# One pair of w_out products spread over both halves of the array around a batch's kv, and 32 columns of numerators in a round of their own

## The chip, the cores and the metric

The kernel runs on one core of a Trainium2 chip. The metric is the device time of one execution in microseconds (us), the median of the runs. Engines: TensorE (PE, with its weight loads as PEld), VectorE (DVE), ScalarE (ACT), GpSimd (POOL) and SyncE (SP, here only DMA issues).

## The reference: linear attention, then a gated feed-forward block

For each of 4 batches and 4 heads, 1088 tokens of 32 dimensions: q and k are mapped by two sketches S1 and S2 (8 rows each) to a = S1 x and b = S2 x, and phi(x) holds their 64 products. Then

```
kv  = sum over s of phi(k) v          # 64 x 32 a head
z   = sum over s of phi(k)            # 64 a head
out = (phi(q) kv) / (phi(q) z + 1e-6)
x   = out, as 4352 tokens x 128
y   = (sigmoid(x w_gate) * (x w_val)) w_out     # 128 -> 1536 -> 128
```

All is in f32.

## The kernel before, in words

**The feed-forward block is the stream that runs through the kernel.** The 4352 tokens are cut into chunks of 512 (`tok_chk`), the hidden 1536 into 12 blocks of 128. A *wave* (`w1`, L529 to L605) makes one block's gate and value products for one chunk in a PSUM tile `wave` (two buffers): from chunk 1 on each of the two is split into two products of 64 output rows (L542 to L544), so that two run side by side in the two halves of the array, one in its low 64 columns and one in its high 64. ACT takes the sigmoid (L552), and `glu` multiplies on DVE (L587). `slot` (L613) is the planner: for each wave it first finishes the wave before it (`glu`), then does the w_out products that are due (`todo`, due 3 and 4 waves after their pair), then issues the next wave. The calls from L1314 to the end write out by hand between which waves the attention's steps of the next batch stand, by wave numbers in `plan`.

**The w_out products.** From chunk 1 on, two hidden blocks form a pair (i = 0 to 5), and a 2 by 2 scheme with seven products replaces eight: POOL makes sums of the token halves (`token_sums`, tile `tsum`), `ws` holds sums of weights. `w2_a` (L468) issues three or four products of a pair into PSUM bank `fst["a"]`, one wave later `w2_b` (L495) the rest, mostly into bank `fst["b"]`. All have 64 output rows: `lo` is rows 0 to 63 of a bank and runs in the low half of the array, `hi` is rows 64 to 127 and runs in the high half; the rhs has 256 columns (`HALF`). For an even pair `w2_a` issues lo (L475), hi (L476), lo (L477); `w2_b` lo, hi, lo, hi. For an odd pair `w2_a` issues lo, hi, lo, hi and `w2_b` hi, lo, hi. So an even pair's first round gives the low half one product more, and the odd pair's second round gives it back to the high half. The products of a round stand right ahead of a wave on PE.

**The attention of batches 1 to 3**, each step between two waves: `begin` (kps, cqps: the sketches of k and q), `outer` and `sum_z` on DVE (phi(k) and its sum), then `kv_all` (L1310): 36 products of 64 columns and 4 more for z, in four groups of 32 output rows, over the whole array (L900, L909). In batch 1, kv stands between pair 0's `w2_a`, one wave, and pair 0's `w2_b`. Later `parts(b)` (L1276) makes numerators and denominators:

- `den_j` (L1026): eight products of 160 columns into the PSUM tile `denj` (buffer "two", one of its kind). The operands have 64 rows and the output 32, so that eight tiles of the array (two row halves, four column groups) work side by side. Between them stand eight numerator products of the last 32 columns, into the same tile at columns 160 to 191.
- DVE multiplies the sums by A8 into `pd` (L1047).
- eight numerator products of 512 columns into `nps`, a `wave` buffer (L1280 to L1282), copied out by ACT (L1285).
- `den_i` (L1051): two products of 160 columns from `pd` back into `denj`, whose columns 0 to 159 pd has read by then.
- DVE turns and inverts the denominators (`turn_den`) and multiplies the numerators by them into xT (L1302), the 32 last columns from `denj`.

Of the kernel before, what the change touches and what calls it, by code (L numbers as in the profile page):

```python
# [8 lines left out]
F32 = mybir.dt.float32  # L9
# [7 lines left out]
P = 128  # L17
# [3 lines left out]
def kernel(  # L21
# [12 lines left out]
    nc = tc.nc  # L34

    B, H, S, D = q.shape
# [26 lines left out]
    ps2 = ctx.enter_context(tc.tile_pool(name="ps2", bufs=1, space=bass.MemoryType.PSUM))  # L63
# [13 lines left out]
    W1 = 32 * q_chk[1][1]  # L77
# [111 lines left out]
    HALF = TCH // 2  # L189
    ws = const.tile([P, 4, NJ // 2, 64], F32, tag="ws", name="ws")  # L190
# [129 lines left out]
    for c in range(2):  # L320
        rows = slice(64 * c, 64 * c + 64)
        nc.vector.tensor_reduce(
            out=m_col[rows, c],
# [4 lines left out]
    for t, x in (  # L328
# [5 lines left out]
        out=e_sum,  # L334
# [45 lines left out]
    def product(out, lhsT, rhs, start, stop):  # L380
        nc.tensor.matmul(  # L381
            out=out, lhsT=lhsT, rhs=rhs, start=start, stop=stop, skip_group_check=True
        )
# [78 lines left out]
    fst = {}  # L462
# [2 lines left out]

    def w2_a(ci, i, g, t):  # L468
        if i == 0:
            moe["sum"] = ci  # L470
            fst["a"] = pso.tile([P, TCH], F32, tag="acc0", name="prod")
        ps = fst["a"]
        lo, hi = ps[:64], ps[64:]
        w, first, last = w_sb[:, 2], i == 0, i == NJ // 2 - 1
        product(lo[:, :HALF], w[:, 2 * i, :64], g[:, 0, :HALF], first, last)  # L475
        product(hi[:, :HALF], ws[:, 1, i], t[:, 2], first, last)  # L476
        product(lo[:, HALF:], ws[:, 3, i], g[:, 1, HALF:], False, last)  # L477
        if i % 2:
            product(hi[:, HALF:], ws[:, 2, i], t[:, 1], False, last)
        if last:  # L480
            e = fst["e"] = raw.tile([P, 4, HALF], F32, tag="w_in", name="other")
            r = fst["r"] = raw.tile([P, 3, HALF], F32, tag="w_in", name="res")
            nc.scalar.copy(out=e[:64, 0], in_=hi[:, :HALF])
            nc.scalar.copy(out=e[64:, 0], in_=lo[:, :HALF])  # L484
            add(r[:, 0], ps[:, :HALF], e[:, 0])
            add(r[:, 0], ps[:, HALF:], r[:, 0])
            moe["copies"] += [
                lambda: nc.scalar.copy(out=e[:64, 1], in_=lo[:, :HALF]),
                lambda: nc.scalar.copy(out=e[64:, 1], in_=r[64:, 0]),
            ]  # L490
# [4 lines left out]
    def w2_b(ci, i, g, t):  # L495
        if i == 0:
            fst["b"] = pso.tile([P, TCH], F32, tag="acc1", name="prod")
        ps = fst["b"]
        lo, hi = ps[:64], ps[64:]
        w, first, last = w_sb[:, 2], i == 0, i == NJ // 2 - 1  # L500
        p5 = (lo[:, HALF:], ws[:, 0, i], t[:, 0], False, last)
        p4 = (hi[:, :HALF], w[:, 2 * i + 1, 64:], t[:, 3], first, last)
        out2 = hi[:, HALF:] if i % 2 else lo[:, :HALF]
        p2 = (out2, w[:, 2 * i + 1, :64], g[:, 1, :HALF], first, i >= NJ // 2 - 2)
        p7 = (fst["a"][64:, HALF:], ws[:, 2, i], t[:, 1], False, False)
        for p in (p4, p5, p2) if i % 2 else (p2, p7, p5, p4):
            product(*p)
        if last:
            e, r = fst["e"], fst["r"]
            nc.scalar.copy(out=e[:64, 3], in_=hi[:, HALF:])  # L510
            o_sb = sbA.tile([P, TCH // 32, 32], F32, tag="o_sb", name="o_sb")

            add(r[:, 1], ps[:, :HALF], e[:, 1])
            add(r[:64, 1], r[:64, 1], e[:64, 3])
            moe["copies"] += [
                lambda: nc.scalar.copy(out=e[:64, 2], in_=lo[:, HALF:]),
                lambda: nc.scalar.copy(out=e[64:, 2], in_=lo[:, HALF:]),
            ]

            def turn_store():  # L520
                nc.vector.transpose(
                    out=o_sb.rearrange("p t x -> p (t x)"),
                    in_=r[:, 1:3].rearrange("p u x -> p (u x)"),
                )
                store(ci, lambda g4: o_sb[32 * g4 : 32 * g4 + 32])

            moe["late"] += [lambda: add(r[:, 2], r[:, 0], e[:, 2]), turn_store]
# [140 lines left out]
    WD = 160  # L668
# [352 lines left out]
        )  # L1021

    def den_j(b):  # L1026
        t = ps2.tile([P, 2, 512], F32, tag="two", name="denj")
        rest = t[:, :, WD : WD + 32]

        def sum_j(pi, x):  # L1030
            rows = slice(64 * pi, 64 * pi + 64)
            nc.tensor.matmul(  # L1032
                out=t[32 * x : 32 * x + 32, pi, :WD],
                lhsT=ZW[b][rows, 4 * (x % 2) : 4 * (x % 2) + 4].rearrange("p x i -> p (x i)"),
                rhs=B8[b][rows, (W1 - WD) * (x // 2) : (W1 - WD) * (x // 2) + WD],
                start=True,
                stop=True,
            )

        for x in range(4):  # L1040
            sum_j(0, x)
            numerator(b, rest, x, 1, True)
        for x in range(4):
            sum_j(1, x)
            numerator(b, rest, x, 0, True)
        PD[b] = sbA.tile([P, 2, WD], F32, tag="pd", name="pd", bufs=1)
        nc.vector.tensor_tensor(out=PD[b], in0=t[:, :, :WD], in1=A8[b], op=MUL)  # L1047
        return t


    def den_i(b, dps):  # L1051
        for pi in range(2):
            nc.tensor.matmul(  # L1053
                out=dps[64 * pi : 64 * pi + 64],
                lhsT=mask["head"].rearrange("p m x -> p (m x)"),
                rhs=PD[b][:, pi, :],
                start=True,
                stop=True,
            )
        return dps  # L1060

    def turn_den(b, dps):
        nt, over = WD // 32, (W1 - WD) // 32
        dT = sbA.tile([P, nt, 32], F32, tag="dTi", name="dTi", bufs=1)
        nc.vector.transpose(out=dT.rearrange("p t c -> p (t c)"), in_=dps)
        RC[b] = sbA.tile([P, 2, W1 // 32, 2], F32, tag="rci", name="rci")
        for t0, t1, u0, k in ((0, nt, 0, 0), (nt, W1 // 32, nt - over, 4)):
            nc.vector.tensor_scalar_add(
                RC[b][:, :, t0:t1],
                dT[:, u0 : u0 + t1 - t0, k : k + 4].rearrange("p t (n c) -> p n t c", n=2),  # L1070
                1e-6,
            )
        nc.vector.reciprocal(out=RC[b], in_=RC[b])
# [79 lines left out]
    else:  # L1153
        nc.vector.tensor_copy(
            out=s4[:, 1:],
# [106 lines left out]
        glu()  # L1262
        late.append(dn(0, 1)(later=True))

    def numerator(b, t, h, c, rest):
        rows = slice(64 * c, 64 * c + 64)
        q1 = QP[b].rearrange("p (n h w) -> p n h w", n=2, h=H)[rows, :, 2 * (h % 2) + h // 2]
        nc.tensor.matmul(  # L1268
            out=t[32 * h : 32 * h + 32, c],
            lhsT=ND[b][rows, 32 * h : 32 * h + 32],  # L1270
            rhs=q1[:, 1, W1 - 32 :] if rest else q1[:, :, : W1 - 32],
            start=True,
            stop=True,
        )

    def parts(b):  # L1276
        t2 = den_j(b)
        glu()
        t = psm.tile([P, 2, 512], F32, tag="wave", name="nps")
        for h in range(H):  # L1280
            for c in range(2):
                numerator(b, t, h, c, False)  # L1282
        num = sbA.tile([P, 2, NJK, 2, F], F32, tag="kp", name="num", bufs=1)
        num = num.rearrange("p c j m f -> p (c j m f)")[:, :1024].rearrange("p (c w) -> p c w", c=2)
        nc.scalar.copy(out=num, in_=t)  # L1285
        turn_den(b, den_i(b, t2[:, 0, :WD]))
        for n in range(2):
            rb = sbA.tile([P, 9, 2, 32], F32, tag="rb", name="rb")
            t0, tn = q_chk[n]
            r0 = RC[b][:, n]  # L1290
            nc.vector.transpose(
                out=rb[:, :tn].rearrange("p t c s -> p (t c s)"),
                in_=bass.AP(
                    tensor=r0.tensor,
                    offset=r0.offset,
                    ap=[list(r0.ap[0]), [1, 2 * tn], [0, 32]],
                ),
            )
            for u0, u1, x in ((0, 8, num[:, :, 256 * n : 256 * n + 256]), (8, tn, t2[:, :, WD : WD + 32])):
                if u0 < u1:  # L1300
                    o = b * S + 64 * (t0 + u0)
                    nc.vector.tensor_tensor(  # L1302
                        out=xT[:, o : o + 64 * (u1 - u0)].rearrange("p (t c s) -> p c t s", c=2, s=32),
                        in0=x.rearrange("p c (t s) -> p c t s", s=32),
                        in1=rb[:, u0:u1].rearrange("p t c s -> p c t s"),
                        op=MUL,
                    )
        moe["ready"] = b * S + S
# [102 lines left out]
```

## Time and profile before

| what | value |
|---|---|
| median of 3 runs | 290.91 us (290.83 to 291.48) |
| the profiled execution's own time | 291.36 us |
| its span, first to last instruction | 289.3 us |
| PE busy | 283.5 us, 98% of the span |
| POOL, DVE, ACT busy | 159.6, 170.8, 106.6 us |
| granted TensorE clock | 1.00 |
| waves (L544), 820 records | 201.9 us, mean 566 ns |
| w_out products (L381), 588 records | 168.6 us, 379 to 380 ns each |

An f32 product leaves two records, one for each of two passes over its columns. A record's duration holds the time from a pass's start until its last result; the next pass on the same part of the array starts earlier than that, so the distance between starts is what a pass occupies. Records of the two halves overlap in time, which is why the two lines' busy times add up to more than the span. A timeline row with a count (x7) merges records of one line that follow each other.

### The profile page before, as it was taken

Reading aid. Unit: us, or ns where it says so; the run is one execution under the profiler, and the core shown is the slowest. Engines: PE = TensorE matmul, PEld = TensorE weight load, DVE = VectorE, ACT = ScalarE, POOL = GpSimd, SP = SyncE. Lnnn points to the kernel's source line nnn. Section 1 sums busy time; section 2 is a strip of 40 time slices with the busy share of each in tenths; the row PEclk is TensorE's granted clock in tenths of the full one; section 3 lists DMA queues with packets and bytes.
Section 4 is the critical chain, followed back from the end, with each engine's and each line's share of the span. In section 5 each row is a group of like instructions: output and inputs, shape, how many; then the busy total and the mean of one; then the engine's idle time right before and its main releaser. Section 6 shows DMA issues by size and latency. Waiting matters only on the chain.

```text
span 289.3 us, 5786 instructions
## 1 busy us (share of the span) xinstructions
PE 283.5 (98%) x2260; PEld 134.9 (47%) x2260; DVE 170.8 (59%) x294; ACT 106.6 (37%) x215; POOL 159.6 (55%) x222
## 2 busy tenths in 40 slices
PE   8799999999999999999999999999999999999995
PEld 4454433354444444544444444444444444444685
DVE  6987788946738547668346385767245223522571
ACT  3688833222334322533234222522243223421341
POOL 2566673667466377372665396483564646555200
PEclk9999999999999999999999999999999999999999
DMA  7995541665600386442000683010001100020012
GB/s 216 343 361 120 111 155 42 164 147 135 186 11 2 77 187 162 105 156 37 0 1 6 157 162 128 2 28 10 0 3 18 18 2 0 3 35 1 0 17 40
DMA packets 28890, 24.22 MB, mean 84 GB/s; under 512 B 18560, under 2 KB 24064, under 8 KB 28864
## 3 DMA queue, kind: packets, MB, share of 16 engines
q1 hardware_dynamic: 25888, 22.10, 30.1%
q10 hardware_dynamic: 2976, 1.77, 2.1%
q8 instruction: 17, 0.28, 0.4%
q14 instruction: 9, 0.07, 0.1%
HBM read 20.60 MB, written 3.26 MB: 82 GB/s over the span
## 4 chain that ended last, share of the span: by engine, by line
PE 97%; ACT 1%; DVE 1%; issue 0%; POOL 0%
PE wave L544 61%; PE prod L381 22%; PE moeout L425 4%; PE moeout L451 2%; PE warm L301 2%; PE kvz L900 1%; PE nps L1268 1%; PE kps L681 1%; PE cqps L827 1%; PE nps L1101 0%; PE dps L1082 0%; PE denj L1053 0%; PE denj L1032 0%; ACT asb L798 0%; DVE qp L807 0%; PE ndps L965 0%
## 5 line engine op out<-in xcount | busy, mean ns | idle before, releaser
L544 PE MATMUL wave<-xT,w_sb 128*64 128x512 f32 (+3 forms) x820 | 201.9, 566 | 0.0
L552 ACT ACTIVATE sg<-wave 128x512 f32<-128x512 f32 x102 | 60.9, 597 | 158.6 <-PE wave L544 152.6
L587 DVE TENSOR_TENSOR g<-wave,sg 128x512 f32<-128x512 f32 x96 | 66.1, 688 | 88.2 <-ACT sg L552 87.6
L371 POOL TENSOR_TENSOR tsum<-g,tsum 128x256 f32<-128x256 f32 x84 | 68.4, 815 | 71.6 <-DVE g L587 71.5
L544 PEld LDWEIGHTS wave<-xT,w_sb 128*64 128x64 f32 (+1 forms) x820 | 71.3, 140 | 72.8 <-issue 53.0
L371 POOL TENSOR_TENSOR tsum<-g 128x256 f32<-128x256 f32 x84 | 66.4, 791 | 22.6 <-DVE g L587 22.0
L381 PE MATMUL prod<-tsum,ws 128*64 128x256 f32 x252 | 68.3, 380 | 0.0
L381 PE MATMUL prod<-g,w_sb 128*64 128x256 f32 x168 | 50.2, 380 | 0.0
L381 PEld LDWEIGHTS prod<-tsum,ws 128*64 128x64 f32 x252 | 34.0, 137 | 13.1 <-issue 9.7
L381 PEld LDWEIGHTS prod<-g,w_sb 128*64 128x64 f32 x168 | 22.7, 137 | 30.0 <-issue 25.8
L381 PE MATMUL prod<-tsum,w_sb 128*64 128x256 f32 x84 | 25.1, 380 | 0.0
L381 PE MATMUL prod<-g,ws 128*64 128x256 f32 x84 | 25.0, 379 | 0.0
L162 POOL TENSOR_TENSOR head<-head,tail 128x384 int32<-128x384 int32 (+1 forms) x13 | 13.2, 1021 | 4.4 <-DVE head L157 4.4
L381 PEld LDWEIGHTS prod<-g,ws 128*64 128x64 f32 x84 | 11.5, 137 | 5.7
L425 PE MATMUL moeout<-g,w_sb 128*128 128x512 f32 (+1 forms) x28 | 12.4, 600 | 0.0
L381 PEld LDWEIGHTS prod<-tsum,w_sb 128*64 128x64 f32 x84 | 11.3, 137 | 1.3 <-issue 1.0
L760 DVE TENSOR_TENSOR kp<-kab 128x1152 f32<-128x1152 f32 (+2 forms) x10 | 10.7, 1082 | 0.0
L580 DVE TENSOR_TENSOR g<-wave,sg 128x512 f32<-128x512 f32 x6 | 7.0, 1172 | 6.1 <-ACT sg L552 4.6
L880 DVE TENSOR_TENSOR qp<-qp,bq 128x1152 f32<-128x1152 f32 (+1 forms) x7 | 10.1, 1444 | 0.0
L493 DVE TENSOR_TENSOR res<-prod,other 128x256 f32<-128x256 f32 x14 | 6.0, 425 | 6.3 <-ACT other L484 4.8
L141 POOL TENSOR_SCALAR head<-cap 128x384 f32<-128x384 f32 (+1 forms) x13 | 6.3, 487 | 5.0 <-ACT cap L140 5.0
L152 ACT ACTIVATE tail<-w_in,two__157 128x384 f32<-128x384 uint32 (+1 forms) x12 | 7.3, 614 | 0.0
(132 smaller groups left out, 200.2 us busy)
## 6 DMA issues: line engine op xcount, KB each, us to landing
qp<-dq SPq DMA_DIRECT2D x7, 576.0 KB
bq<-dq SPq DMA_DIRECT2D x14, 288.0 KB
kq<-in_k_dram SPq DMA_DIRECT2D x3, 544.0 KB
kq<-in_q_dram SPq DMA_DIRECT2D x3, 544.0 KB
w_in<-in_moe_w_out_dram SPq DMA_DIRECT2D x6, 256.0 KB
w_in<-in_moe_w_gate_dram SPq DMA_DIRECT2D x5, 256.0 KB
w_in<-in_moe_w_val_dram SPq DMA_DIRECT2D x5, 256.0 KB
v<-in_v_dram SPq DMA_DIRECT2D x8, 144.0 KB
```

The costliest lines, as they stand in the source:

```text
L141: nc.gpsimd.tensor_scalar(out=self.head.bitcast(F32), in0=self.cap, scalar1=122880.0, scalar2=2.0**-15, op0=ALU.min, op1=ALU.max,)
L152: nc.scalar.activation(out=self.tail, in_=self.lo, func=ACTF.Identity, bias=two, scale=2.0**-51)
L162: nc.gpsimd.tensor_tensor(out=self.head, in0=self.head, in1=self.tail.bitcast(I32), op=ALU.add)
L371: nc.gpsimd.tensor_tensor(out=t[:, u], in0=in0, in1=in1, op=ALU.subtract)
L381: nc.tensor.matmul(out=out, lhsT=lhsT, rhs=rhs, start=start, stop=stop, skip_group_check=True)
L425: nc.tensor.matmul(out=moe["acc"][d], lhsT=w_sb[:, 2, j, d], rhs=g[:, jj], start=(j == 0), stop=(j == NJ - 1),)
L544: nc.tensor.matmul(out=wv[d, which, jj * tw + o : jj * tw + o + tp], lhsT=w_sb[:, which, j0 + jj, d], rhs=xT[:, t0 + o : t0 + o + tp], sta ...
L552: nc.scalar.activation(out=sg, in_=wv[:, 0], func=ACTF.Sigmoid)
L580: nc.vector.tensor_tensor(out=g.rearrange("p (j u s y) -> p j y u s", j=2, u=2, y=4), in0=wv[:, 1].rearrange("p (j y u s) -> p j y u s", j ...
L587: nc.vector.tensor_tensor(out=g, in0=wv[:, 1], in1=sg, op=MUL)
L760: eng.tensor_tensor(out=KP[b][:, pi, j0:j1].rearrange("p j m (i l) -> p (j m) i l", i=R), in0=bass.AP(tensor=a0.tensor, offset=a0.offset, ...
L880: nc.vector.tensor_tensor(out=q0, in0=q0, in1=half(BQ[b], n), op=MUL)
```

## The change

In `w2_a` the third product (L477) is left out for pair 0 of chunk 1. In `w2_b` that pair gets an order of its own: p2, the product into `lo[:, :HALF]`, is cut into two pieces of 128 columns, the second of which goes to the high half (`hi[:, HALF + x:]`, which is added to the low half's result at the end in any case), and the left-out product p3 is issued here, into `fst["a"]`. In `parts`, the eight numerator products of 32 columns no longer stand between the sums of `den_j`: they come after the 512-column numerators and their copy, in a new tile of the buffer "two", which `den_i` then writes too.

```diff
@@ w2_a
-        product(lo[:, HALF:], ws[:, 3, i], g[:, 1, HALF:], False, last)
+        if ci > 1 or i > 0:
+            product(lo[:, HALF:], ws[:, 3, i], g[:, 1, HALF:], False, last)
@@ w2_b
-        for p in (p4, p5, p2) if i % 2 else (p2, p7, p5, p4):
+        order = (p4, p5, p2) if i % 2 else (p2, p7, p5, p4)
+        if ci == 1 and i == 0:
+            w21, x = w[:, 1, :64], HALF // 2
+            p3 = (fst["a"][:64, HALF:], ws[:, 3, 0], g[:, 1, HALF:], False, False)
+            p2s = [
+                (lo[:, :x], w21, g[:, 1, :x], True, False),
+                (hi[:, HALF + x :], w21, g[:, 1, x:HALF], False, False),
+            ]
+            order = (p2s[0], p7, p3, p4, p5, p2s[1])
+        for p in order:
             product(*p)
@@ den_j
-        for x in range(4):
-            sum_j(0, x)
-            numerator(b, rest, x, 1, True)
-        for x in range(4):
-            sum_j(1, x)
-            numerator(b, rest, x, 0, True)
+        for pi in range(2):
+            rows = slice(64 * pi, 64 * pi + 64)
+            for x in range(4):
+                nc.tensor.matmul(...)
@@ numerators (was numerator, one product a call)
+    def numerators(b, t, rest):
+        for h in range(H):
+            for c in range(2):
...
@@ parts
-        t2 = den_j(b)
+        den_j(b)
         glu()
         t = psm.tile([P, 2, 512], F32, tag="wave", name="nps")
-        for h in range(H):
-            for c in range(2):
-                numerator(b, t, h, c, False)
+        numerators(b, t, False)
...
         nc.scalar.copy(out=num, in_=t)
-        turn_den(b, den_i(b, t2[:, 0, :WD]))
+        t = ps2.tile([P, 2, 512], F32, tag="two", name="nps2")
+        numerators(b, t[:, :, WD : WD + 32], True)
+        turn_den(b, den_i(b, t[:, 0, :WD]))
...
-            for u0, u1, x in (..., (8, tn, t2[:, :, WD : WD + 32])):
+            for u0, u1, x in (..., (8, tn, t[:, :, WD : WD + 32])):
```

The sum products in `den_j` and the numerator products themselves are the same as before; only their places and the tile of the 32-column ones differ.

More of the change, by code (lines that the diff above doesn't have):

```diff
@@ L1027, in den_j @@
         t = ps2.tile([P, 2, 512], F32, tag="two", name="denj")
-        rest = t[:, :, WD : WD + 32]
-        def sum_j(pi, x):
+        for pi in range(2):
             rows = slice(64 * pi, 64 * pi + 64)
[L1032 to L1038, printed above, removed]
-        for x in range(4):
-            sum_j(0, x)
-            numerator(b, rest, x, 1, True)
-        for x in range(4):
-            sum_j(1, x)
-            numerator(b, rest, x, 0, True)
+            for x in range(4):
+                nc.tensor.matmul(
+                    out=t[32 * x : 32 * x + 32, pi, :WD],
+                    lhsT=ZW[b][rows, 4 * (x % 2) : 4 * (x % 2) + 4].rearrange("p x i -> p (x i)"),
+                    rhs=B8[b][rows, (W1 - WD) * (x // 2) : (W1 - WD) * (x // 2) + WD],
+                    start=True,
+                    stop=True,
+                )
         PD[b] = sbA.tile([P, 2, WD], F32, tag="pd", name="pd", bufs=1)
         nc.vector.tensor_tensor(out=PD[b], in0=t[:, :, :WD], in1=A8[b], op=MUL)
-        return t
     def den_i(b, dps):
@@ L1263, in part01 @@
         late.append(dn(0, 1)(later=True))
[L1265 to L1274, printed above, removed]
+    def numerators(b, t, rest):
+        for h in range(H):
+            for c in range(2):
+                rows = slice(64 * c, 64 * c + 64)
+                q1 = QP[b].rearrange("p (n h w) -> p n h w", n=2, h=H)[rows, :, 2 * (h % 2) + h // 2]
+                nc.tensor.matmul(
+                    out=t[32 * h : 32 * h + 32, c],
+                    lhsT=ND[b][rows, 32 * h : 32 * h + 32],
+                    rhs=q1[:, 1, W1 - 32 :] if rest else q1[:, :, : W1 - 32],
+                    start=True,
+                    stop=True,
+                )
     def parts(b):
-        t2 = den_j(b)
+        den_j(b)
         glu()
         t = psm.tile([P, 2, 512], F32, tag="wave", name="nps")
-        for h in range(H):
-            for c in range(2):
-                numerator(b, t, h, c, False)
+        numerators(b, t, False)
         num = sbA.tile([P, 2, NJK, 2, F], F32, tag="kp", name="num", bufs=1)
@@ L1298, in parts @@
             )
-            for u0, u1, x in ((0, 8, num[:, :, 256 * n : 256 * n + 256]), (8, tn, t2[:, :, WD : WD + 32])):
+            for u0, u1, x in ((0, 8, num[:, :, 256 * n : 256 * n + 256]), (8, tn, t[:, :, WD : WD + 32])):
                 if u0 < u1:
```

## The prediction

> **What bounds the kernel now.** I read the page first: busy times, then the chain that ended last.
>
> ```profile
> PE 283.5 (98%) x2260; PEld 134.9 (47%) x2260; DVE 170.8 (59%) x294; ACT 106.6 (37%) x215; POOL 159.6 (55%) x222
> ...
> PE 97%; ACT 1%; DVE 1%; issue 0%; POOL 0%
> ```
>
> TensorE (PE) is busy 98% of the span and carries 97% of the chain; no other engine reaches 60%. The list of PE's own waits then says where it ever stood still: five rows, 2.6 us together, all in the first 15 us (warm, dps, ndps, nps, gram). After that PE waits for nobody as a whole. What can be lost is idle **parts** of the array: a product of 64 output rows fills one half (a record 128*64), a 32-row tile one of four column groups, and a busy PE may have the other half idle. So each edit is priced by the order of PE's records.
>
> First place, around batch 1's kv (timeline of PE; start, duration, what):
>
> ```profile
> 56.10 0.59 PE L544 MATMUL wave<-xT,w_sb 128*64 128x512 f32 x1
> 56.32 0.38 PE L381 MATMUL prod<-g,ws 128*64 128x256 f32 x1
> 56.53 1.89 PE L544 MATMUL wave<-xT,w_sb 128*64 128x512 f32 x7
> 58.35 1.21 PE L900 MATMUL kvz<-kp,v 128*32 128x64 f32 x72
> 59.38 0.29 PE L909 MATMUL kvz<-zs,const-float32-1.0 128*32 128x64 f32 x8
> 59.60 0.43 PE L381 MATMUL prod<-g,w_sb 128*64 128x256 f32 x1
> ```
>
> Each f32 product leaves two records (two passes); passes in one half follow each other every 0.215 us for 256 columns (55.67, 55.88) and every 0.429 for 512. L477's third product of pair 0 occupies the low half from 56.11 to 56.53 (its second pass is the row at 56.32) while the high half has begun the wave at 56.10. So the low half runs one product, 0.43 us, behind: the wave's records start in pairs up to 57.39/57.40, and the eighth starts alone at 57.83 and streams until 58.26. The high half is done at 57.82 and idles until kv, which starts at 58.35 in all four column groups. That is the lost time: 0.43 us of half an array.
>
> Second place, the denominators and numerators of batch 1 (batches 2 and 3 look the same, from 129.35 and 193.57):
>
> ```profile
> 72.80 1.27 PE L1268 MATMUL nps<-qp,nd 64*32 64x512 f32 x16
> 74.00 0.49 PE L1053 MATMUL denj<-pd,head 128*64 128x160 f32 x4
> 74.32 0.38 PE L381 MATMUL prod<-g,w_sb 128*64 128x256 f32 x1
> ```
>
> and on VectorE (DVE):
>
> ```profile
> 73.21 0.49 DVE L1047 TENSOR_TENSOR pd<-denj,a 128x320 f32<-128x320 f32 x1 [1.83 <-PE denj L1032]
> 73.62 0.68 DVE L587 TENSOR_TENSOR g<-wave,sg 128x512 f32<-128x512 f32 x1
> ```
>
> The stage runs from 72.44 (first denj record) to 74.00 (den_i): 1.56 us, in all three batches. Its columns per tile are 160 + 32 + 512, two passes each, at 0.84 ns a column: 1.18 us. The last nps pass starts at 73.48 and streams 0.43 to 73.91; 0.09 later den_i starts, the same 0.09 that separates wave and denj where the tile shape changes. So den_i waits for the array to empty, not for pd, which ends at 73.70. The remaining 0.29 us is lost in the mixed start: the upper row tiles get their first sum at 72.60 though they could take it at about 72.49, and all nps tiles but one begin at 72.93 to 73.03.
>
> **Part 1, the balanced pair.** The third product (two passes of 256) leaves w2_a and moves behind kv. Low and high half then both end the wave at 57.83, and kv starts 0.43 us earlier. What kv needs is there: two of its waits for the v loads were passed at 55.7 to 55.8, and only bq, a and b are in flight between 55 and 58.4, kp is older, and zs (DVE, done at 57.90) is first needed by the last four products, at about 58.95. Behind kv the round grows from four products to the equivalent of five: low half 128 + 256 + 256 columns, high half 256 + 256 + 128, two passes each: 1.07 us a half where it was 0.86. That costs 0.21. No half waits for the other: start times in the low half are 0, 0.21, 0.64, in the high half 0, 0.43, 0.86, rising in program order. The 128-column passes cost no more than their columns: ndps at L965 has such passes every 0.109 us (64.81, 64.92, then the next product at 65.03). tsum's slices for p7 and p4 were ready at 57.63 on GpSimd, 1.5 us before they are needed. Gain 0.43 - 0.21 = **0.22**; bounds 0.43 (the added product lands in idle columns) and 0.11 (each of the two new pieces starts like the first record after kv, 430 instead of 380 ns).
>
> [...] In this trace the second product after kv starts at 59.61, while the first product's second pass starts at 59.87.
>
> **Part 2, the round of its own.** Eight products of 32 columns per batch leave den_j and come behind the 512-column ones; the count stays. They write a new tile in the same PSUM buffer, so the first of them takes over den_i's wait for pd (L1047). Behind it in PE's queue stand only the other seven and den_i; the next w_out products and the wave shift with them. DVE, ScalarE, GpSimd and SP have the same instructions in the same order, DMAs included; nothing is moved past a queue of theirs.
>
> Row for the new start: kps and cqps (L681, L827), eight tiles of 64*32 in two passes, begin 7 ns apart and each pass follows the last without loss (47.27, 47.51 for 288 columns). So, from the stage's start: denj second passes start at 0.16 to 0.21, nps first passes at 0.29 to 0.34, second ones by 0.79, end 1.22 (up to 1.29 at the 17 ns spacing that nps shows now); it is 1.47 today. pd: the last denj pass ends at 0.21 + 0.30 = 0.51, DVE starts 0.14 later as today, takes 0.49: 1.14, and PE sees it 0.11 later, as dps (L1082) saw zb (11.12 to 11.23): 1.25, or 1.31 with the wider spacing. **The wait for pd is thus what is late next**, by some hundredths; I take 1.28. Then the 32-column round and the change of tile shape: the 64*32 pair of gram takes 0.176 from start to the next shape (8.21 to 8.38), and seven more tiles at 7 ns make 0.22. den_i starts at 1.50 instead of 1.56: **0.06 gained per batch, 0.18 in all**. Bounds per batch: +0.11 gained (everything at the early end) and 0.11 lost (pd at 1.31, sixteen passes 17 ns apart, 0.27, then 0.09). So 0.33 either way.
>
> **Sum.** 0.22 + 0.18 = 0.40. The profiled execution took 291.36 (span 289.30 and 2.06 around it), so it would become 290.96; the median of the three runs, 290.91, lies 0.45 lower, and with the same difference becomes **290.51**. Nothing downstream takes it back: chunk 2's first wave, at 82.50, needs batch 1's xT, done at 78.79.
>
> **Rivals.**
> - A, only part 1 pays: the den stage comes out even. 290.91 - 0.22 = 290.69. For it: pd ends only 0.2 before den_i today.
> - B, everything at its good end: 0.43 + 0.33 = 0.76, 290.15. It needs the added product to cost nothing; PE's record gives no idle half behind kv, so unlikely.
> - C, slower: the new wait takes the place of the lost start. If denj's last sum is no earlier than now, pd ends at 73.70, PE sees it at 73.81; weights that could not be loaded ahead cost 0.05 (den_i's first record has 350 against 299 ns), sixteen passes at 17 ns 0.27, the last pass 0.03, the drain 0.09: den_i at 74.25, 0.25 late, three times 0.75; with part 1 at 0.11 the total is +0.64, 291.55. It decides once the round begins more than 0.07 us after the 1.28 above at row spacing. Against it: without the numerators between, the last sum is the eighth of PE's instructions instead of the fifteenth.
> - D, the change doesn't do what it says: kv's start is held by something else at 58.35, and the moved product adds its 0.21. 290.91 + 0.21 - 0.18 = 290.94. Against it: no wait of PE in that list.
>
> **Numbers.** Forecast 0.50, A 0.20, B 0.10, C 0.12, D 0.08. The range runs from near B to between D and C, taking in part 1's and part 2's bounds (0.11 gained and 0.33 lost is +0.22, 291.13): 290.10 to 291.20. What a measurement of this kernel can tell from no change is about 0.2%, 0.58 us: faster means below 290.33, which is B (0.10); slower above 291.49, half of C (0.06); the rest, 0.84, is within it.
>
> **What would show it.** After: the wave before kv ends in a pair, kv about 0.43 earlier, the round behind it 1.07 long. The den stage 1.50 long, with den_i no longer waiting for pd and the 32-column tile doing so. Wrong if the eighth wave record still starts alone, if the wait list of PE gains a row for the new tile of over 0.1 us a batch, or if the 32-column round takes over 0.3 us.

## The result, and the profile after

| | before | after |
|---|---|---|
| median of 10 runs, taken side by side | 291.24 us | 290.12 us (289.84 to 290.45) |
| ratio after to before, 95% interval | | 0.9959 (0.9941 to 0.9976) |
| the profiled execution: time, span | 291.36, 289.3 us | 289.88, 288.1 us |

The ratio leaves out one run of before in the slow state (296.05 us, which is in its median). The change makes the kernel faster, by 0.24% to 0.59%; the two medians differ by 1.12 us. The forecast was 290.51, 0.40 us below the 290.91 that was known then; the direction was right, the size was not.

First the page of the kernel after: busy times, and the engines' shares of the chain that ended last.

```profile
PE 282.3 (98%) x2262; PEld 134.4 (47%) x2262; DVE 171.2 (59%) x294; ACT 106.7 (37%) x215; POOL 159.7 (55%) x222
...
PE 97%; ACT 1%; DVE 1%; issue 0%; POOL 0%
```

Nothing has changed in what bounds the kernel. PE has two records more (one product more, from the cut) and is busy 1.2 us less. The list of PE's own waits has the same five rows as before (warm, dps, ndps, nps of L1102, gram; 2.5 us instead of 2.6), and no row for the new tile. So once more everything must be read from the order of PE's records.

**Around batch 1's kv.** PE's timeline of the kernel after; first a narrow window at the end of the wave ahead of kv, then the round behind kv (start, duration, what).

```profile
56.93 0.60 PE L556 MATMUL wave<-xT,w_sb 128*64 128x512 f32 x2
57.46 0.26 PE L912 MATMUL kvz<-kp,v 128*32 128x64 f32 x4
```

```profile
58.72 0.32 PE L381 MATMUL prod<-g,w_sb 128*64 128x128 f32 x1
58.72 0.43 PE L381 MATMUL prod<-tsum,ws 128*64 128x256 f32 x1
58.88 0.27 PE L381 MATMUL prod<-g,w_sb 128*64 128x128 f32 x1
...
59.63 0.38 PE L381 MATMUL prod<-tsum,ws 128*64 128x256 f32 x1
59.64 0.38 PE L381 MATMUL prod<-g,w_sb 128*64 128x128 f32 x2
59.85 1.03 PE L556 MATMUL wave<-xT,w_sb 128*64 128x512 f32 x4
```

The two last records of the wave now start together: two passes that merge into one row of 0.60 us, where one pass alone takes 0.59. Kv follows 0.53 after that start, as it followed 0.52 after the lone record. Behind kv both halves begin at 58.72 and both begin the next wave at 59.85; in the kernel with the pair left as it was (below) this round lasts from 59.13 to 60.05. So the round is 0.22 longer (1.132 where it was 0.915). From the records: batch 1's first kps to kv takes 11.155 us instead of 11.587 (0.432 less), kv to ndps 6.684 instead of 6.465 (0.219 more). **Part 1 gains 0.213 us.**

**The den stage of batch 1.** PE's timeline and DVE's, both of the kernel after.

```profile
71.24 0.60 PE L556 MATMUL wave<-xT,w_sb 128*64 128x512 f32 x2
71.77 0.50 PE L1041 MATMUL denj<-b,zw 64*32 64x160 f32 x16
72.07 1.16 PE L1271 MATMUL nps<-qp,nd 64*32 64x512 f32 x32
73.15 0.49 PE L1054 MATMUL nps<-pd,head 128*64 128x160 f32 x4
```

```profile
72.38 0.49 DVE L1049 TENSOR_TENSOR pd<-denj,a 128x320 f32<-128x320 f32 x1 [1.23 <-PE denj L1041]
72.79 0.68 DVE L599 TENSOR_TENSOR g<-wave,sg 128x512 f32<-128x512 f32 x1
```

In the kernel before, sixteen alternating rows stood ahead of the first 512-column product; now there is one. The 512-column products start right behind the sums (72.07, 0.30 into the stage), and the 32-column round is merged into the same row (x32: 16 passes of 512 and 16 of 32 columns). Den_i starts at 73.15: the stage lasts 1.382 us where it lasted 1.561, and it does so in all three batches (1.382, 1.383, 1.382). **Part 2 gains 0.179 us a batch, 0.536 in all.**

**The sum.** 0.213 + 0.536 = 0.749 us. Everything else between these places agrees in the two traces to 2 ns (batch 2's kps to kv 18.479 and 18.478, the last den_i to PE's last product 90.639 and 90.640). The two spans differ by 1.20, though: the remaining 0.45 lies ahead of batch 1's first kps (46.76 us after the first record before, 46.31 after), where the two kernels have the same code. It is looked at under the last experiment.

### The profile page after: what moved, and what is told of

Its sections match the earlier page's. It is cut to its first block, busy times and chain, and to the rows that moved or that the text cites. A ratio compares the mean times of both kernels' runs of the same rounds, so it can differ in the third digit from the quotient of the medians.

```text
span 288.1 us, 5789 instructions
## 1 busy us (share of the span) xinstructions
PE 282.3 (98%) x2262; PEld 134.4 (47%) x2262; DVE 171.2 (59%) x294; ACT 106.7 (37%) x215; POOL 159.7 (55%) x222
## 3 DMA queue, kind: packets, MB, share of 16 engines
q10 hardware_dynamic: 2976, 1.77, 2.1%
## 4 chain that ended last, share of the span: by engine, by line
PE 97%; ACT 1%; DVE 1%; issue 0%; POOL 0%
PE wave L556 61%; PE prod L381 22%; PE moeout L425 4%; PE moeout L451 2%; PE warm L301 2%; PE kvz L912 1%; PE nps L1271 1%; PE kps L693 1%; PE cqps L839 1%; PE nps L1102 0%; PE denj L1041 0%; PE dps L1083 0%; PE nps L1054 0%; ACT asb L810 0%; DVE qp L819 0%; PE aps L800 0%
## 5 line engine op out<-in xcount | busy, mean ns | idle before, releaser
L371 POOL TENSOR_TENSOR tsum<-g,tsum 128x256 f32<-128x256 f32 x84 | 67.5, 804 | 71.0 <-DVE g L599 70.8
L371 POOL TENSOR_TENSOR tsum<-g 128x256 f32<-128x256 f32 x84 | 67.5, 804 | 22.3 <-DVE g L599 21.7
L381 PE MATMUL prod<-g,w_sb 128*64 128x256 f32 (+1 forms) x170 | 50.3, 378 | 0.0
```

The source lines that it names most:

```text
L371: nc.gpsimd.tensor_tensor(out=t[:, u], in0=in0, in1=in1, op=ALU.subtract)
L381: nc.tensor.matmul(out=out, lhsT=lhsT, rhs=rhs, start=start, stop=stop, skip_group_check=True)
```

## The experiments

Distances between landmarks are read from the records of the trace, in us; "stage" is from the first denj record to den_i. "kps" is the first record of a batch's sketch of k, "ndps" that of the step on PE that takes up kv's result (L965 of the kernel before).

**The kernel before once more.** No edit.

> The kernel before, unchanged, as a control. Theory (the change gives 0.21 at kv and 0.18 in each of three den stages, 0.75 in all, and the other 0.45 of the 1.20 between the two profiles is start-up that differs from execution to execution): ratio 1.000 with an interval that holds 1, den stages of 1.56, kv preceded by a lone wave record; the first kps record may start anywhere from 5.9 to 6.4 us, as it did at 6.29 in before and 5.96 in after. Rival (the earlier start belongs to the changed kernel): first kps record at 6.29 again, within 0.05.

Measured: 291.16 (ratio 1.0005, 0.9992 to 1.0018); landmarks 11.587, 6.465, stages 1.560 to 1.561. The landmarks repeat to 1 ns from execution to execution. The first kps is at 6.32 us and batch 1's at 46.92, 0.16 later than in the other trace of the same kernel. A first kps at 6.32 fits the theory and the rival alike, so this run doesn't tell them apart; the last experiment does.

**Part 1 alone.** The kernel before with the edits in `w2_a` and `w2_b` only.

> Only the balanced pair; the den stage as before. Theory: kv starts 0.43 earlier measured from kps of batch 1, the stretch from kv to ndps is 0.21 longer, den stages stay 1.56; 0.21 faster, ratio 0.9993. Rival (the start-up gain comes with the change): 0.21 + 0.45, ratio 0.9977 and the first kps record near 5.96.

**Part 2 alone.** The kernel before with the edits in `den_j`, `numerators` and `parts` only.

> Only the 32-column round of its own; the pair as before. Theory: den stage 1.38 in all three batches, kv still preceded by a lone wave record; 0.54 faster, ratio 0.9981. Rival (start-up comes with this part): 0.54 + 0.45, ratio 0.9966. By the prediction on record 0.18 faster, ratio 0.9994.

Measured:

| | time | ratio (95%) | kps to kv | kv to ndps | stage |
|---|---|---|---|---|---|
| part 1 alone | 290.52 | 0.9987 (0.9978 to 0.9995) | 11.155 | 6.683 | 1.561 |
| part 2 alone | 290.63 | 0.9980 (0.9968 to 0.9991) | 11.587 | 6.465 | 1.381 to 1.383 |
| both | 290.12 | 0.9959 (0.9941 to 0.9976) | 11.155 | 6.684 | 1.382 |

The parts do not touch each other, and each has in its own kernel the landmarks that it has in the changed one. Part 1 is worth what the forecast said, part 2 three times as much. The rivals' ratios, 0.9977 and 0.9966, lie just outside the two intervals, though the first kps stood early in both traces (6.01 and 5.95 us).

**The round put back ahead of the 512-column products, but behind the sums.** The kernel after, with the 32-column products in `denj` again:

```diff
@@ den_j, behind the eight sums
+        numerators(b, t[:, :, WD : WD + 32], True)
@@ parts, behind the copy
-        t = ps2.tile([P, 2, 512], F32, tag="two", name="nps2")
-        numerators(b, t[:, :, WD : WD + 32], True)
+        t = t2
```

> The kernel after, but the 32-column products stand between the eight sums and the 512-column products, in the tile denj; only den_i waits for pd. Theory (the loss before came from numerators standing between sums; the place of the round matters little): den stage 1.35 to 1.42, time equal to after within 0.2 us. Rival (the gain comes from the round's place behind the 512-column products): den stage 1.50 or more, 0.35 us or more slower than after.

Measured: stages 1.560 to 1.561, those of the kernel before; 290.52 us, ratio to before 0.9995 (0.9973 to 1.0017). The theory is refuted, the rival met. PE's timeline of this kernel, the second half of the stage (which begins at 71.83), and below it the same place in the kernel before (stage from 72.44):

```profile
72.12 0.25 PE L1273 MATMUL denj<-qp,nd 64*32 64x32 f32 x13
72.19 0.59 PE L1273 MATMUL nps<-qp,nd 64*32 64x512 f32 x1
72.19 0.21 PE L1273 MATMUL denj<-qp,nd 64*32 64x32 f32 x3
72.32 1.14 PE L1273 MATMUL nps<-qp,nd 64*32 64x512 f32 x15
73.39 0.36 PE L1056 MATMUL denj<-pd,head 128*64 128x160 f32 x2
```

```profile
72.80 0.59 PE L1268 MATMUL nps<-qp,nd 64*32 64x512 f32 x1
72.80 0.19 PE L1268 MATMUL denj<-qp,nd 64*32 64x32 f32 x1
72.93 1.14 PE L1268 MATMUL nps<-qp,nd 64*32 64x512 f32 x15
```

The sums run in perfect order here, and it helps nothing: one 512-column product starts at 72.19 (0.356 into the stage), the other seven only from 72.32 (0.491 to 0.591), although the last short pass has begun by 0.371 and streams 0.03. The same hole stands in the kernel before (72.80, then 72.93). So the alternation among the sums was not the loss. The loss is this hole ahead of the second 512-column product, with the wider starts behind it (17 ns apart instead of 7), and it goes when the short products stand behind. The weight loads have the hole too: those of the 512-column products start at 0.326, 0.358 and then 0.487, 4 ns ahead of the second product, and only the first of them carries a semaphore wait. So the loads stop as well, and no wait for another engine is recorded in the hole.

**The round without its wait.** The 32-column products write `denj` right behind the 512-column ones, and pd is formed after them, with `glu()` behind it; den_i stays in `denj` too:

```diff
@@ den_j
-        PD[b] = ...
-        nc.vector.tensor_tensor(out=PD[b], in0=t[:, :, :WD], in1=A8[b], op=MUL)
@@ parts, behind numerators(b, t, False)
+        numerators(b, t2[:, :, WD : WD + 32], True)
+        PD[b] = ...
+        nc.vector.tensor_tensor(out=PD[b], in0=t2[:, :, :WD], in1=A8[b], op=MUL)
```

> The kernel after, but the 32-column round writes the tile denj and does not wait for pd (den_i does). If the round of after starts when the first tile of the 512-column products is free (1.15 us into the stage) and not when pd arrives: stage 1.38 as in after, within 0.02. If the wait for pd sets its start: the round starts earlier and the stage is shorter by over 0.03.

Measured: 292.61 us, stage 2.183. My premise failed: pd, now the later instruction, waited for the last product that writes its tile, so that it starts 1.64 into the stage instead of 0.61, and den_i waits for it. PE's timeline of this kernel (stage from 72.11):

```profile
73.26 0.27 PE L1270 MATMUL denj<-qp,nd 64*32 64x32 f32 x16
74.29 0.36 PE L1053 MATMUL denj<-pd,head 128*64 128x160 f32 x2 [0.76 <-DVE pd L1284]
```

One reading stands in spite of that: the round, which waits for nobody here, starts 1.154 into the stage. With its wait, in the kernel after, it starts at 1.156. What differs is the weight loads. Without the wait the first eight of the round start at 0.727 to 0.773, while the 512-column products still run, and its sixteen passes start within 0.075 us. In the kernel after no weight load of the round starts before 1.155, and the passes need 0.104.

**The wait made late.** The kernel after with `glu()` moved from behind `den_j` to ahead of pd, so that a 0.68 us product on DVE stands in front of it:

> The kernel after, but on VectorE the glu product of 0.68 us stands ahead of pd, so pd ends later. If the round's wait for pd has next to no slack in after: pd ends some 0.8 later, the stage is longer by 0.70 to 0.80 in each batch, and the whole 2.1 to 2.4 us slower than after; PE's wait list gains a row for the new tile of 2 us or more in all. If the wait has slack of over 0.2: less than 0.6 a batch.

Measured: 292.70 us in one execution (2.6 above the median of after), stages 2.124, 2.186, 2.185; the new row of PE's wait list is 1.7 us in all, less than expected. PE's timeline (stage from 72.16):

```profile
74.06 0.30 PE L1272 MATMUL nps<-qp,nd 64*32 64x32 f32 x16 [0.54 <-DVE pd L1050]
74.29 0.49 PE L1055 MATMUL nps<-pd,head 128*64 128x160 f32 x4
```

The round follows pd's end (1.843) by 0.055 us, and the stage is 0.74 to 0.80 longer. The wait is real and has no slack: in the kernel after pd ends at 1.103, the round's first weight load starts 0.052 later, at 1.155 (0.053 with the late pd), and the first tile is free at 0.725 + 0.429 = 1.154. The round starts at 1.156. The two conditions come true within 2 ns of each other.

**The round ahead of the sums.** The `numerators` call of the kernel with the round put back, moved ahead of the loop over `pi`.

> The kernel after, but the 32-column round stands first, ahead of the eight sums. [...] Theory T (whatever follows a 32-column product on its tile starts some 0.13 us late): a gap of 0.1 between the round and the sums, stage 1.45 to 1.52.

Measured: 290.61 us, stages 1.532, 1.532, 1.549. The lower sums follow their short products without a hole (0.129 to 0.149, behind second passes at 0.052 to 0.099), but the upper four start only at 0.264 and after (no first pass of theirs stands in the records between 0.149 and 0.264). So a hole comes here too, after the twelfth product and not the seventeenth, and theory T's stage was not met.

**Half of the round ahead, half behind.** Four 32-column products (c = 0) behind the sums, the other four behind the 512-column ones, all in `denj`.

> The kernel after, but four of the eight 32-column products (c = 0) stand between the sums and the 512-column products, the other four behind them. [...] Theory T (a short product delays its follower): a gap of some 0.13 us right after the first 512-column product, as in the kernel with all eight there, and first passes 17 ns apart.

Measured: 290.36 us, stages 1.555 to 1.556. Five 512-column products start right behind the short ones, on used and unused tiles alike (0.323, 0.330, 0.356, 0.363, 0.370), then comes the hole, and the last three follow at 0.492, 0.509 and 0.525. That a product behind a short one on its own tile starts late (theory T) is refuted. What is the same in three kernels is the count and the time: the hole stands behind the seventeenth product of the stage (8 + 8 + 1 twice, 8 + 4 + 5 here), and the eighteenth starts at 0.491 or 0.492, the next ones 17 ns apart.

**Sixteen long products ahead.** Count and time are told apart by making the products in front longer. The kernel after with the sums issued twice:

```diff
@@ den_j
-        for pi in range(2):
+        for pi in (0, 1, 0, 1):
```

> The changed kernel, with the eight sums of 160 columns of a stage issued twice (the second set writes the same values again), so that sixteen products stand ahead of the 512-column ones as before the change, but sixteen that take longer. Sums cost 0.269 us (two passes of 160 columns at 0.84 ns). [...] Rival (count: the gap of 0.12 us stands behind the seventeenth product whatever the products last): the first 512-column product alone, the others 0.12 us behind it, stage 1.77 us.

Measured: 291.34 us, stages 1.654 in all three. PE's timeline (stage from 72.41):

```profile
72.41 0.77 PE L1041 MATMUL denj<-b,zw 64*32 64x160 f32 x32
72.98 1.16 PE L1271 MATMUL nps<-qp,nd 64*32 64x512 f32 x32
74.07 0.36 PE L1054 MATMUL nps<-pd,head 128*64 128x160 f32 x2
```

The 512-column products start at 0.567 to 0.614, 7 ns apart, without a hole behind the seventeenth product, and the rival's 1.77 is not met: the stage is 0.272 longer, the price of the added columns. So it is not the count alone. Sixteen products that last until 0.57 to 0.61 cost only their columns, sixteen that are through by 0.40 cost a hole until 0.49. Nor is it a fixed time: with the short products first the hole ended at 0.264.

**The row halves exchanged.** The kernel before; each 32-column product stands behind the sum of the same row half (`numerator(b, rest, x, 0, True)` in the first loop, `1` in the second).

> The kernel before, with the 32-column numerators of the two row halves exchanged in the list: each now stands behind the sum of the same row half, not of the other one. Theory (the number of short products ahead of the 512-column ones makes the gap, not which tiles they alternate between): the stage is 1.56 us as before, with the second to eighth 512-column products again from 0.49 us on. Rival (the alternation between row halves makes the loss): the stage is changed by more than 0.1 us either way.

Measured: stages 1.605 in all three (the time of this one execution, 293.89 us, says nothing about the edit: PE's mean granted clock was 0.986, and batch 1 began 2.4 us late; from 14.2 us on, long ahead of the stages, the granted clock is 1.00). Neither side was met: the stage grows by 0.044, less than the rival's 0.1 and not the theory's nothing. The hole is there (one 512-column product at 0.356, one at 0.512, the rest from 0.552, 17 ns apart), a little later. The order among the short products counts for some hundredths.

**The pair without the cut.** The kernel after, p2 whole:

```diff
@@ w2_b
-            order = (p2s[0], p7, p3, p4, p5, p2s[1])
+            order = (p2, p7, p3, p4, p5)
```

> The changed kernel, but p2 of the pair isn't cut: the round behind kv is p2, p7, p3 to the one half as they come and p4, p5, so that the low half has three products of 256 columns and the high half two. Theory (the halves are evened out only because of the cut): kv stands 0.43 us earlier as after the change (kps to kv 11.155 us), the round behind kv leaves the low half 0.43 us behind, the waves up to batch 1's denominators start in staggered pairs, and the wave ahead of the denominators (or of ndps) ends in a lone record; from kv to the denominators it takes 0.21 us longer than after the change, so the whole of part 1's 0.21 us is lost again and the kernel stands at the time of the one with the round alone (body 0.53 to 0.54 us below before). Rival (the cut costs as much as it evens out): the same from kv to the denominators as after the change, within 0.05 us. The den stages stay at 1.38 us in both.

Measured: 291.14 us in one execution; kps to kv 11.155, kv to ndps 6.522 (0.162 less than after), ndps to denominators 7.995 (0.368 more), stages 1.381 to 1.383. The low half's third product is carried along as a lag and is paid where the array must be even again. PE's timeline ahead of batch 1's denominators, and for comparison that of the kernel after, each in a narrow window:

```profile
71.40 1.45 PE L552 MATMUL wave<-xT,w_sb 128*64 128x512 f32 x5
72.78 0.34 PE L1037 MATMUL denj<-b,zw 64*32 64x160 f32 x4
```

```profile
70.39 1.46 PE L556 MATMUL wave<-xT,w_sb 128*64 128x512 f32 x6
71.77 0.35 PE L1041 MATMUL denj<-b,zw 64*32 64x160 f32 x5
```

An odd number of passes, five, in the last 1.45 us: a lone record at the end, as there had been before kv. One half starts its last pass at 71.88 and the other at 72.26, 0.37 later. The net is 0.206 lost, all that part 1 gains. The product that is moved only moves the idle half; it is the cut that removes it.

**The kernel after once more.** No edit.

> The changed kernel once more, unedited. Theory (the change is worth 0.213 us at the pair and 0.179 us in each of three stages, 0.75 us in all, and the rest of the first comparison's difference of spans is the start-up, which differs between executions whatever the kernel): the ratio of the medians is 0.9974, in an interval that takes this in; kps to kv 11.155, kv to ndps 6.684, the stages 1.38. Rival (the change speeds up the start as well, 1.2 us in all): ratio 0.9959 or below, and the first kps again at 5.95 us.

Measured: 289.95 us, ratio 0.9959 (0.9946 to 0.9973); landmarks 11.155, 6.683, stages 1.381 to 1.383. The first kps is at 6.19 us and batch 1's at 46.53. The 0.749 us of the landmarks make 0.9974, which lies inside the first comparison's interval and by 0.0001 outside this one: the theory's ratio was not met. But neither does the start-up belong to the change: kernels with the same code up to batch 1 reach its first kps anywhere from 46.27 to 47.11 us, and the first kps of the program at 5.92 to 6.35 (the one execution at clock 0.986 left out). PE's first records, in the timeline of the kernel before and of the kernel after:

```profile
5.57 0.79 PE L301 MATMUL warm<-const-float32-1.0 128*128 128x128 f32 x2
6.29 0.81 PE L681 MATMUL kps<-kT,sk 64*32 64x288 f32 x16
```

```profile
5.52 0.49 PE L301 MATMUL warm<-const-float32-1.0 128*128 128x128 f32 x2
5.96 0.72 PE L693 MATMUL kps<-kT,sk 64*32 64x288 f32 x16
```

The two passes of the same last warm-up product (two records) take 0.79 and 0.49 us here, 0.80 in the kernel before once more and 0.74 in the kernel after once more. The records say why: PE starts at half the pace of the waves. The first 512-column passes of the program stand 0.853 us apart, twice the 0.429 of the waves, and the moment at which PE speeds up differs between executions of the same code. The page's row PEclk doesn't show it; the trace's first record of a granted clock of 1.00 begins at 6.58 us in before, 6.87 in before once more, 5.48 in after and 6.08 in after once more. In six traces (the one at clock 0.986 left out again) the two passes of the last warm-up product start 0.212 or 0.213 us apart, and the first kps stands at 5.92 to 6.02; in seven they start 0.373 to 0.375 apart, and it stands at 6.19 to 6.35. From there to batch 1's kps it takes 40.34 to 40.35 us where the clock record begins by 6.31, and 40.45 to 40.60 where it begins at 6.50 or later. Both traces of before happened to be late ones, which makes the 0.45 us between the two profiles. (In the kernel with the pair uncut that stretch takes 41.10 at an early clock; this cause is open.)

The spans of all runs have medians of 288.9 and 289.0 for before (35 and 11 runs), 288.7 for either part alone and 288.25 and 288.1 for both (10 and 6 runs). For both parts that is 0.65 to 0.9 less, which fits the landmarks; part 2 alone shows less than its 0.536. About 0.1 us lies outside the span (1.93 and 1.94 for before beside 1.82 and 1.83 for after), and it is not the change's: the kernel before once more also had 1.82. What remains between 0.75 and the measured 1.0 to 1.2, some 0.25 to 0.45 us with that 0.1 in it, is open: how often PE speeds up late is not known for the runs without a trace.

## Why the prediction was wrong, point by point

- **Kv 0.43 earlier: right.** 0.432. The wave ends in a pair; nothing else held kv, so D falls.
- **The round behind kv 0.21 longer: right.** 0.219. Its whole length is 1.13, not 1.07, but it was 0.92 and not 0.86 before: the first 256-column pass behind kv takes 0.267 from start to start, not 0.215, in both kernels. The net of part 1 was forecast at 0.22 and is 0.213.
- **"No half waits for the other": right.** From 58.717 on, the low half's products start at 0, 0.27 and 0.70 us and the high half's at 0.01, 0.49 and 0.92, where 0, 0.21, 0.64 and 0, 0.43, 0.86 were forecast; the 0.05 to 0.06 more comes from the first pass in each half (0.160 for 128 columns and 0.267 for 256, from start to start). P7 starts at 58.723, ahead of the second pass of the first piece of p2, at 58.877: here the product in one half was not held up by the other half's product in front of it.
- **Part 2, 0.06 a batch: wrong in size; this is the step that failed.** The forecast let the round begin at 1.28, midway between pd seen at 1.25 and at 1.31, behind the last tile's end at 1.22. It begins at 1.156. Two terms were too long. The round does not need the array to be empty, it needs its own tile: the first one is free at 1.154, and the round's first products run while the last 512-column passes still stream (these end at 0.772 + 0.429 = 1.20; the forecast's own row, 0.34 + 0.43, gives a second pass by 0.77 and not 0.79, so 1.20 as well). And pd is seen at 1.155 and not at 1.25: it starts 0.108 after the last sum instead of 0.14, and PE starts 0.052 after its end instead of 0.11. From its start on the step was right: the round and the change of tile shape take 1.382 - 1.156 = 0.226 where the forecast had 0.22, from a row whose weights were not loaded ahead either. So 1.28 against 1.156 is the whole of the 0.12 a batch that was missed, and the bound of 0.11 gained was too narrow for the same reason: it was built on the same start (and 1.25 + 0.22 makes it 0.09, not 0.11).
- **"The wait for pd is what is late next": half right.** It is late at the same instant as the tile, so the round's first product loses 2 ns by it, and it has no slack. But it also holds the round's weight loads, and the passes then need 0.104 us where the round without its wait needs 0.075: some 0.03 us a batch, an estimate from these two rows. The forecast had such a price, 0.05, in C.
- **"The remaining 0.29 us is lost in the mixed start": wrong reading.** With the sums in order and the short products behind them the stage is still 1.561. What was lost was a hole behind the seventeenth product (0.135 us from start to start in the kernel before, 0.12 with half of the round ahead) and starts 17 ns apart behind it. So the move helped for a reason that the forecast didn't have.
- **Rivals.** A (part 2 comes out even) and C (the wait for pd takes over) are refuted by the stage of 1.382; C's mechanism exists, as the late pd showed at 0.74 to 0.80 a batch, but its condition, a round that begins more than 0.07 behind 1.28, was off by 0.2. B's 0.76 is nearly the measured 0.75, but by another split: it wanted 0.43 and 0.33, and the landmarks give 0.213 and 0.536: its total is near by luck.

## What to carry to other kernels

The round of 32 columns, a step that is cut into tiles of the array, did not begin when the array was empty but when its own tile was free (at 1.156 us, with the first tile free at 1.154 and the last at 1.20), and only the change of tile shape came behind the last tile (by 0.09): price a round like this one by its own tile and a change of shape by the last. An odd number of half-array products ahead of a full-array step cost one product's time here, 0.43 us, and moving it only moved the idle half: count both halves up to every such step. Short products did better behind the long ones: eight of them in front cost 0.18 us a stage more than behind.

## What the runs showed of the hardware

- **Behind a burst of short products PE started the next ones late.** In three kernels (before, the round put back, half of it put back) the first seventeen products of the stage have started by 0.37 us, the eighteenth starts at 0.491 to 0.492 and the next ones 17 ns apart, where the kernel after takes its free tiles 7 ns apart; with 16 products of 160 columns in front nothing is lost. With the short products first a hole came already behind the twelfth, and it ended at 0.264. The cause is open.
- **A change of tile shape cost 0.09 us** at three places of the kernel after or before: wave to denj 0.093 (71.250 + 0.429 to 71.772), 512-column nps to den_i 0.089 before, 32-column round to den_i 0.095. Each is counted from the end of the last tile's columns: at these places the new shape did not start before that.
- **The start-up of the same code varies** by 0.4 us up to the first kps and by 0.8 up to batch 1, more than the whole change, while the landmarks behind it repeat to 2 ns. The 0.4 goes with the moment at which PE leaves the pace of its first products (0.853 us a pass of 512 columns, later 0.429): the trace's first full-clock record begins anywhere from 3.96 to 6.90 us. Differences of this size are read from landmarks, not from spans.
